# A Fourier layer and two MLPs on one core: conversions one step earlier, forward folds on VectorE, and more of the inverse split in halves

## The chip, the cores and the metric

The kernel runs on one core of a Trainium2 chip. The metric is the time of one execution on the device in microseconds; three runs of the kernel before stand below, and one profiled execution from which all rows come. The core's engines are TensorE (PE; its weight loads PEld), VectorE (DVE), ScalarE (ACT) and GpSimd (POOL); SyncE (SP) and GpSimd issue the DMAs. They work side by side and wait for each other through semaphores; each works through its own queue in order.

## What is computed

The input is two sequences of 3008 tokens with 256 channels, in float32. A Fourier transform over the tokens is followed by a complex 256x256 product, a bias, a soft threshold, and the inverse transform; its output goes through two MLPs, 256 to 2048 to 256, with float64 arithmetic nowhere but in the weights' storage.

```python
X = np.fft.rfft(x, axis=1)
Yr = Xr @ w_r - Xi @ w_i + b_r
Yi = Xr @ w_i + Xi @ w_r + b_i
Yr = np.sign(Yr) * np.maximum(np.abs(Yr) - 0.01, 0.0)    # Yi too
y = np.fft.irfft(Y, n=x.shape[1], axis=1)
h = y @ w_in;  g = h * sigmoid(1.702 * h);  z = g @ w_out
h = z @ w_in2; g = h * sigmoid(h);          out = g @ w_out2
```

## The kernel before

The program has four stages in a row.

**Forward** (`groups`, 16 steps g): the rfft as matrix products. The tokens are folded first: sums and differences of mirrored tokens (`fold`), so that the matrices shrink. A group (q, b, t) is a parity q of the sample, a batch b, and t, in which t // 2 is the parity of the frequency and t % 2 is cosine or sine. `fold(g + 3)` makes the operands `xf` of a later group: first `lv` (L309, 128x512) where t < 2, then `xf` or `dd` (L320, 128x256), and for q = 1 a further half (L329). `E(site, i)` picks the engine for each, V or P, from a string in CFG by index: in `lv` 5 and 11, in `dd` 10 and in `pr` 3 are P. `load_m` issues a group's matrix on SP, `load_raw` the next raw tiles. `fwd_mm(g)` multiplies (L361) and `fwd_evac` copies the result out of PSUM one step later.

**Middle** (`mids`, 12 steps i): the complex product (`mid_mm`: the first two in float32, L518, the others in three passes of rounded operands, L521, which need `wh` and `wl`, made at L502 and L503), then the threshold and the folds for the inverse.

**Inverse** (16 steps, 8q + 4b + t): `inv_mm` multiplies (L361, `psi`), `inv_post` adds and subtracts halves one step later. Where `split_sums` is true for a matrix, its rows are split into even and odd: two half-wide products give sums and differences, one copy on ScalarE (L648) and two adds on VectorE (L391, L656) join them. Where it isn't, ScalarE copies both banks (L643). CFG's `eo` has four digits for four matrices; the last is that of odd samples and even frequencies.

**MLPs** (two layers l, six blocks i of 1024 tokens, eight steps p each): `group` makes the hidden values of a pair of tiles by seven products (L818) with sums between (L837 and L853, L855 on ScalarE; L839, L863, L866 on VectorE), gates them (L821, L823, L828), and `out_next` adds the down products (L790) one step late. Between them it calls `hook(1)` to `hook(6)`.

The weights come as float64 bit patterns and are converted on the chip, in the order of `WEIGHTS`: `cv_load` fetches raw bits (SP; one buffer), `cv_bits` makes ScalarE's L175 and puts five VectorE operations (L180 to L184) and an accumulating DMA on GpSimd's queue (L185) into `fill`, which `pump` issues. The tile `cv_c` (tag `c`) has one buffer: the next L175 waits until that DMA has read it. `settle` collects what is converted; `place_in` and `place_out` (through `window`) split it into a rounded part and a rest (L105 to L110). Where these run is a list: `tf` steps of the forward stage, `tm` and `ml` of the middle, `ti` (convert) and `pl` (place) of the inverse, `kb` for the eight steps of the first MLP block and `kr` for later ones. Layer 0's sixteen pieces stay in SBUF; layer 1's are converted during later blocks, written to DRAM and fetched again.

Orders: in the forward stage GpSimd and SP keep program order and a planner orders the other engines; from the middle stage on all engines keep program order. PSUM has two pools of four banks.

Of the kernel before, what the change touches and what calls it, by code (L numbers as in the profile page):

```python
# [8 lines left out]

F32 = mybir.dt.float32  # L10
CFG = {'lv0': 'V', 'lv': 'VVVVVPVVVVVP', 'dd0': 'VPVVPPPPPVVP', 'dd': 'VVVVVVVVVVPV', 'ths': 'VVVVPV', 'thf': 'VVVP', 'ivf': 'V', 'cva': 'P', 'pol': 'PPPP', 'pil': 'P', 'mvl': 'PVVP', 'xl': 'V', 'xse': 'V', 'gl': 'VPPPPPPP', 'tf': [6, 9, 11, 14], 'tm': [1, 6, 10], 'ml': [4, 8], 'ti': [8, 11, 14], 'pl': [1, 4, 9, 12, 15], 'kb': [0, 1, 1, 1, 1, 1, 1, 0], 'kr': [0, 1, 0, 1, 0, 1, 1, 0], 'fa': 3, 'xp': [2, 4, 4, 5], 'xq': [1, 4, 1], 'xs': 4, 'xi': [7, 7, 9, 10, 10, 11, 8], 'xsi': 9, 'xo': (0, 1, 6, 2, 3, 4, 5), 'xd': (0, 1, 4, 6), 'ca': 4, 'tl': True, 'fwd': 'Pool,SP', 'rest0': 'all', 'rest1': 'all', 'last1': 'all', 'inv': 'all', 'mid': 'all', 'last0': 'all', 'thm': 'A', 'gl0': 'PVPVVVPV', 'gl2': 'PPPPPPPP', 'gl3': 'PPPPPPPV', 'xl0': 'V', 'xl1': 'V', 'pre': 14, 'pre2': 0, 'yd': 6, 'lvb': 6, 'mlp': 'all', 'pr': 'VVVP', 'pf': 'PV', 'eo': '0110', 'n32': 2, 'li': [8, 10, 11], 'lii': [0], 'xa': 4, 'nhb': 6, 'ddb': 6, 'mlp1': 'all', 'mlp2': 'all'}
NUM = dict(li=[5, 6, 7, 8], n32=2, pk=4, ydp=2, lii=[1, 3], xd=(), ml=[], pl=[], xo=range(7), pi=6, nhb=6, tf=[5, 9, 13], tm=[1, 3, 5, 7, 9, 11], ti=[0, 2, 4, 6, 8, 10, 12, 14, 14, 15, 15], kb=[2] * 8, kr=1, fa=3, fe=2, pm=0, nf=4, lvb=6, ddb=8, ivb=1, eob=1, fsb=6, f1=3, f2=0, fm=[7, 8, 9], fi=[1, 1, 2, 2], pre=13, pre2=1, yd=3, psh=0, ie=[12], xp=[1, 3, 4, 5], xq=[1, 2, 2], xs=5, nw=4, xi=[14, 14, 15, 15], xsi=13, rw=2, ca=4, cc=2, tb=1, tmn=1)

DEF = dict(pr="V", pf="V", lv0="V", lv="VPP", dd0="VVVVVP", dd="VPV", mpl="PV", ths="VP", thf="VVPP", fsl="VP", ivf="PPVV", cva="P", pol="P", pil="P", mvl="V", xl="PPVVPPP", xl0="PPVVPPP", xl1="PPVVPPP", xse="VP", gl="P", gl0="P", gl2="P", gl3="P", wcl="V", thc="V", thm="V")
# [7 lines left out]
P = 128  # L22
# [8 lines left out]
FS = 4  # L31

WEIGHTS = [("in", 0, p, True) for p in range(6)] + [("out", 0, p, True) for p in range(4)]
WEIGHTS += [(kind, 0, p, True) for kind, p in (("out", 4), ("out", 5), ("in", 6), ("in", 7), ("out", 6), ("out", 7))]
WEIGHTS += [(kind, 1, p, False) for kind in ("in", "out") for p in range(8)]

C_HI = float(np.uint32(0x0FEFFEF0).view(np.float32))
# [2 lines left out]
def split_sums(kind, q, p):  # L40
    return (kind, q) == ("f", 0) and CFG.get("eo", "1111")[p] == "1" or (kind, p) == ("i", 0) and CFG.get("eo", "1111")[2 + q] == "1"

# [14 lines left out]
def spectral_mlp_kernel(ctx, tc, xin, mfwd, minv, wc, bias, w_in1, w_out1, w_in2, w_out2, outT):  # L57
# [177 lines left out]
    def settle(now=False):  # L235
        pump()
        for u, (a, c) in bits:
            if not u[3]:
                spilled[u[:3]] = d = dram_p.tile([P, 2 * CU], F32, name=f"w_{u[0]}{u[1]}_{u[2]}")
                nc.sync.dma_start(out=d, in_=a)  # L240
        fresh = [(u, a) for u, (a, _) in bits if u[3]]
        done, added[:] = (added + fresh, ()) if now else (added[:], fresh)
        bits[:] = []
        return done
# [36 lines left out]
    raws, lvs, xs = {}, {}, {}  # L281
# [174 lines left out]

    prev = None
    for g, (q, b, t) in enumerate(groups):
        fold(g + N('fa'))
        ps = fwd_mm(g)  # L460
        if b == B - 1 and m_order[0][0] == "f":
            load_m()
        if prev is not None:
            fwd_evac(*prev)
        prev = (g, ps)
        if g == 6:
            wc_p = opened("wc", "right")
            wc_s = m_p.tile([P, MW], F32, tag="m", name="wc_s")[:, : 6 * D].rearrange("p (k d) -> p k d", k=2)
            bias_hl = wc_p.tile([P, 2 * D], F32R, name="bias_hl")
            bias_lo = wc_p.tile([1, 2 * D], F32R, name="bias_lo")  # L470
            bias_f = wc_p.tile([P, 2 * D], F32, name="bias_f")
            nc.gpsimd.memset(bias_f, 0.0)
            ones = wc_p.tile([P, P], F32R, name="ones")
            ones_f = wc_p.tile([P, P], F32, name="ones_f")

            neglam = wc_p.tile([P, 1], F32, name='neglam')
            nc.vector.memset(neglam, -LAM)


# [432 lines left out]
    done = []  # L912
    added.extend(hold)
    for at, (l, i, p) in enumerate(seq):
        if (l, i, p) in ((0, 0, 1), (0, 0, 2)):
            region(f'mlp{p}')
        if (i, p) == (1, 0):
            region(f'rest{l}')
        if (i, p) == (last, 0):
            region(f'last{l}')  # L920
        nxt = (l, i + 1) if i < last else (1, 0)
        more = p == NPR - 1 and (l, i) != (1, last)
        k = rate(at)

        def hook(h):
            if more:
                if h in (1, 2):
                    for x in ((0,), (1, 2))[h - 1]:
                        xprep(*nxt, x)
                if h == 3:  # L930
                    xprep(*nxt, 3, 1)
                if h == 4:
                    xprep(*nxt, 3, 2)
            if p == 0 and (l, i) != (0, 0):
                for x in {1: (4,), 3: (6, 5)}.get(h, ()):
# [12 lines left out]
            if h == 4:
                pump()
                cv_load(1 - len(loaded))  # L950
            if late and (l, i, p, h) in ((0, 0, 1, 4), (0, 0, 2, 3), (0, 0, 2, 4), (0, 0, 3, 4)):
                kk, y, u, v = late.pop(0)
                (nc.vector.tensor_sub if kk in (0, 3) else nc.vector.tensor_add)(y, u, v)
            if h == 3:
                pump()
                cv_load(1 - len(loaded))
                done.extend(settle())
                done.extend(added)
                added[:] = []
# [146 lines left out]
```

## Time and profile before

| | us |
|---|---|
| runs of the kernel before | 1184.57, 1178.29, 1178.03 |
| their median | 1178.29 |
| profiled execution, whole | 1182.72 |
| its span, first to last instruction | 1180.6 |
| TensorE busy in the span | 1150.5 (97%) |
| ScalarE busy | 773.3 (65%) |
| VectorE busy | 636.1 (54%) |
| GpSimd busy | 502.4 (43%) |

The stages can be read from the lines: the forward stage ends at about 73 us, the middle at about 147, the inverse at about 196; the first MLP block ends near 279. Busy shares are means over stages with different limits, so each stage is read by itself.

### The profile page before, as it was taken

How to read it: one execution, taken by the hardware profiler on the slowest of the kernel's cores; microseconds unless marked ns; L12 is line 12 of the kernel's file. 1: busy time of each engine (PE TensorE's matmuls, PEld its weight loads, DVE VectorE, ACT ScalarE, POOL GpSimd, SP SyncE). 2: the span in 40 equal slices, each digit the busy share in tenths (PEclk: the TensorE clock that was granted, in tenths of full speed). 3: DMA queues.
4: the chain of work that ended last, by engine and by line, in shares of the span. 5: the costliest groups of instructions: out<-in, count | busy, mean ns of one | idle time of the engine just before them, and what ended most of it. 6: DMA issues, size and time to landing. Idle time of an engine off the chain costs nothing.

```text
span 1180.6 us, 14536 instructions
## 1 busy us (share of the span) xinstructions
PE 1150.5 (97%) x5052; PEld 945.3 (80%) x5052; DVE 636.1 (54%) x987; ACT 773.3 (65%) x1439; POOL 502.4 (43%) x430
## 2 busy tenths in 40 slices
PE   7889998999999999999999999999999999999998
PEld 4658885877888888888889978888888888888897
DVE  7768787776556466365564553352532623523522
ACT  2366545777668667667677787675665766766755
POOL 2355254443444444344446755433333433433333
PEclk9989999999999999999999999999999999999999
DMA  7457478432121221121130200010000000000000
GB/s 270 142 128 148 126 148 163 89 80 45 44 64 36 72 63 37 45 72 37 36 89 5 68 10 27 1 37 1 1 36 1 11 26 1 36 1 1 36 1 31
DMA packets 37835, 66.83 MB, mean 57 GB/s; under 512 B 3457, under 2 KB 14977, under 8 KB 37762
## 3 DMA queue, kind: packets, MB, share of 16 engines
q1 hardware_dynamic: 25730, 45.90, 11.9%
q0 software_dynamic: 12032, 20.01, 9.8%
q8 instruction: 39, 0.64, 0.2%
q14 instruction: 34, 0.28, 0.1%
HBM read 35.53 MB, written 10.35 MB: 39 GB/s over the span
## 4 chain that ended last, share of the span: by engine, by line
PE 76%; ACT 3%; DVE 2%; issue 1%; DMA 0%; DVEq 0%; POOL 0%; POOLq 0%
PE o L790 40%; PE x L818 36%; ACT yt L821 1%; DMA wo<-cv_a 0%; ACT x L727 0%; ACT yt L837 0%; DVE yt L839 0%; DVE tmp L213 0%; DVE yt L863 0%; ACT g L823 0%; DVE x L734 0%; ACT yt L855 0%; ACT yt L853 0%; DVE g L828 0%; DVE cv_a L182 0%
## 5 line engine op out<-in xcount | busy, mean ns | idle before, releaser
L828 POOL TENSOR_TENSOR g<-yt,g 128x512 fp32r<-128x512 f32 (+1 forms) x282 | 362.8, 1299 | 491.4 <-PE x L818 337.1
L790 PE MATMUL o<-g,wo 128*128 128x512 f32 (+1 forms) x2304 | 561.0, 386 | 2.6 <-DMA wo<-cv_a 2.6
L818 PE MATMUL x<-x,wi 128*128 128x512 f32 (+1 forms) x2016 | 501.2, 388 | 7.8 <-ACT yt L837 3.1
L790 PEld LDWEIGHTS o<-g,wo 128*128 128x128 f32 x2304 | 433.0, 188 | 83.8 <-DMA wo<-cv_a 3.1
L818 PEld LDWEIGHTS x<-x,wi 128*128 128x128 f32 x2016 | 378.2, 188 | 86.1 <-ACT yt L837 5.4
L821 ACT ACTIVATE yt<-yt 128x512 f32<-128x512 f32 (+1 forms) x288 | 179.1, 622 | 257.1 <-DVE yt L863 205.8
L823 ACT CAST g<-yt 128x512 fp32r<-128x512 f32 (+1 forms) x384 | 235.1, 612 | 12.2
L863 DVE TENSOR_TENSOR yt<-yt,x 128x512 f32<-128x512 f32 (+1 forms) x96 | 64.7, 674 | 217.2 <-PE x L818 216.7
L839 DVE TENSOR_TENSOR yt<-yt,x 128x512 f32<-128x512 f32 (+1 forms) x96 | 64.8, 675 | 167.4 <-ACT yt L837 167.4
L828 DVE TENSOR_TENSOR g<-yt,g 128x512 fp32r<-128x512 f32 (+1 forms) x102 | 70.1, 688 | 72.1 <-ACT g L823 72.1
L361 PE MATMUL psf<-m,xf 128*128 128x190 f32 (+3 forms) x224 | 57.7, 419 | 15.7 <-DVE xf L320 6.5
L361 PEld LDWEIGHTS psf<-m,xf 128*128 128x128 f32 x224 | 41.7, 204 | 31.1 <-POOL xf L320 7.9
L866 DVE TENSOR_TENSOR yt<-yt,x 128x512 f32<-128x512 f32 (+1 forms) x96 | 64.8, 675 | 0.0
L734 DVE TENSOR_TENSOR x<-yt,x 128x512 fp32r<-128x512 f32 (+1 forms) x44 | 46.1, 1047 | 29.7 <-ACT x L727 29.7
L185 POOL DMA_DIRECT2D cv_a<-cv_c x32 | 28.0, 875 | 77.5 <-DVE cv_c L184 61.4
L855 ACT COPY yt<-x 128x512 f32<-128x512 f32 (+1 forms) x96 | 55.8, 581 | 0.7 <-ACT yt L853 0.6
L821 ACT ACTIVATE yt<-x 128x512 f32<-128x512 f32 (+1 forms) x96 | 56.2, 585 | 0.0
L853 ACT COPY yt<-x 128x512 f32<-128x512 f32 (+1 forms) x96 | 55.0, 572 | 0.0
L837 ACT COPY yt<-x 128x512 f32<-128x512 f32 (+1 forms) x96 | 54.8, 571 | 0.0
L361 PE MATMUL psi<-m,f 128*128 128x376 f32 (+3 forms) x208 | 49.9, 396 | 0.0
L361 PEld LDWEIGHTS psi<-m,f 128*128 128x128 f32 x208 | 36.6, 190 | 11.9
L175 ACT ACTIVATE cv_c<-raw 128x512 f32<-128x512 f32 x32 | 21.6, 675 | 27.3 <-DMA cv_a<-cv_c 27.1
(117 smaller groups left out, 834.0 us busy)
## 6 DMA issues: line engine op xcount, KB each, us to landing
raw<-in_wi SPq DMA_DIRECT2D x32, 256.0 KB, 3.5
cv_a<-cv_c POOLq DMA_DIRECT2D x32, 256.0 KB, 5.0
raw<-in_wo SPq DMA_DIRECT2D x16, 512.0 KB, 4.0
raw<-in_x SPq DMA_DIRECT2D x12, 512.0 KB, 4.8
xl<-xt POOLq DMA_DIRECT2D x20, 256.0 KB, 5.5
out_t<-yt SPq DMA_DIRECT2D x20, 256.0 KB, 2.2
m<-in_mi SPq DMA_DIRECT2D x4, 564.0 KB, 9.1
wo<-cv_a POOLq DMA_DIRECT2D x8, 256.0 KB, 5.5
```

The source lines that it names most:

```text
L361: nc.tensor.matmul(ps, hi[:, c : c + P], m[:, k, :w], start=i == 0, stop=i == last)
L790: nc.tensor.matmul(acc[h, mm], st, mv, start=first and k == 0, stop=last and k == 2)
L818: nc.tensor.matmul(ps, st, mv, start=first and m == 0, stop=m == 2, skip_group_check=True)
L821: nc.scalar.activation(g, g if src is None else src, func)
L823: nc.scalar.copy(gh, g)
L828: eng.tensor_sub(gl, g, r32(gh))
L837: nc.scalar.copy(y1, X)
L839: nc.vector.tensor_add(y1, y1, Y)
L853: nc.scalar.copy(y2, Z)
L855: nc.scalar.copy(y3, X)
L863: nc.vector.tensor_add(y2, y2, X)
L866: nc.vector.tensor_add(y3, y3, Z)
```

## The change

Six things, all in the first 285 us or in what is issued there.

- `lv`, `dd` and `pr` become V throughout: three L309, four L320 and two L329 move from GpSimd to VectorE (the early ones of `dd0` stay).
- In the forward loop `fwd_mm(g)` and `load_m` come before `fold(g + 3)`; on SP the matrix load then stands before the raw loads of that fold.
- `eo` is 0111 in place of 0110: the inverse's matrix of odd samples and even frequencies is (4, 188) in place of (3, 376), in steps 8, 9, 12 and 13.
- Conversions: `tm` and `ml` one step earlier, `pk` 6 in place of 4 (a conversion's operations pumped in one middle step), `ti` 5, 8, 11 in place of 8, 11, 14, `pl` with a step 7 more, `kb` one step earlier (its first conversion, that of down piece 4, now in step 0).
- In step 0 of the MLPs that conversion starts at hook 4 in place of 1 and is settled there, so that it can be placed in step 1.
- `WEIGHTS`: down piece 6 before the up pieces 6 and 7.

```diff
-CFG = {'lv': 'VVVVVPVVVVVP', 'dd': 'VVVVVVVVVVPV', 'pr': 'VVVP', 'eo': '0110',
-       'tm': [1, 6, 10], 'ml': [4, 8], 'ti': [8, 11, 14], 'pl': [1, 4, 9, 12, 15],
-       'kb': [0, 1, 1, 1, 1, 1, 1, 0]}
+CFG = {'lv': 'V', 'dd': 'V', 'pr': 'V', 'eo': '0111',
+       'tm': [1, 5, 9], 'ml': [3, 7], 'pk': 6, 'ti': [5, 8, 11], 'pl': [1, 4, 7, 9, 12, 15],
+       'kb': [1, 1, 1, 1, 1, 1, 0, 0]}
...
-WEIGHTS += [(kind, 0, p, True) for kind, p in (("out", 4), ("out", 5), ("in", 6), ("in", 7), ("out", 6), ("out", 7))]
+WEIGHTS += [(kind, 0, p, True) for kind, p in (("out", 4), ("out", 5), ("out", 6), ("in", 6), ("in", 7), ("out", 7))]
...
     for g, (q, b, t) in enumerate(groups):
-        fold(g + N('fa'))
         ps = fwd_mm(g)
         if b == B - 1 and m_order[0][0] == "f":
             load_m()
+        fold(g + N('fa'))
...
-            if h == 1:
+            if h == (1 if at else 4):
                 window(k, ())
...
             if h == 4:
                 pump()
                 cv_load(1 - len(loaded))
+                if at == 0:
+                    done.extend(settle(True))
```

## Rows read from the trace of the kernel before

**Rows 1.** Stages: stretch and its length, busy us (instructions) by engine, clock, DMA

```profile
core 0: us, PE busy (x) PEld busy (x) DVE busy (x) ACT busy (x) POOL busy (x), PEclk, DMA share, GB/s
...
62.00:74.00 12.00, 6.28 (x20) 5.28 (x20) 8.44 (x18) 5.66 (x14) 7.22 (x8) 0.72 0.52 110
74.00:147.00 73.00, 73.00 (x299) 55.45 (x298) 60.14 (x110) 47.94 (x82) 30.35 (x32) 1.00 0.62 135
147.00:196.00 49.00, 49.00 (x213) 36.83 (x212) 40.45 (x75) 23.83 (x46) 25.12 (x25) 1.00 0.83 157
...
285.00:1180.00 895.00, 889.23 (x3984) 746.60 (x3982) 422.14 (x604) 614.23 (x1109) 384.75 (x306) 1.00 0.11 31
```

**Rows 2.** TensorE's waits before 300 us: total, times, longest

```profile
PE psf L361 <- POOL xf L320: 6.2, 3, 5.5
PE x L818 <- ACT yt L837: 3.0, 1, 3.0
PE psf L361 <- DMA m<-in_mf: 2.8, 1, 2.8
PE o L790 <- DMA wo<-cv_a: 2.6, 1, 2.6
```

**Rows 3.** Timeline, forward tail to third middle step: start, us, engine, line [idle before]

```profile
61.24 0.69 ACT L175 ACTIVATE cv_c<-raw 128x512 f32<-128x512 f32 x1 [7.42 <-DMA cv_a<-cv_c]
...
66.92 0.87 POOL L185 DMA_DIRECT2D cv_a<-cv_c  x1 [2.03 <-DVE cv_c L184]
...
68.61 4.75 PE L361 MATMUL psf<-m,xf 128*128 128x188 f32 x14 [5.49 <-POOL xf L320]
...
80.14 1.75 DVE L503 TENSOR_TENSOR wl<-wc_s,wh 128x1536 fp32r<-128x1536 f32 x1
...
86.99 0.80 PE L521 MATMUL psm<-wh,xh 128*128 128x512 f32 x1
```

**Rows 4.** VectorE's folds before 210 us by form: count, busy us, mean ns, idle

```profile
L309 DVE TENSOR_TENSOR lv<-raw 128x512 f32<-128x512 f32 x10 | 6.5, 686 | 0.8 <-DMA raw<-in_x 0.8
...
L320 DVE TENSOR_TENSOR dd<-lv 128x256 f32<-128x256 f32 x8 | 3.0, 420 | 0.1
```

**Rows 5.** Two stretches of the inverse: half-wide forms, then 376-wide ones

```profile
156.00:166.00 10.00, 10.00 (x62) 9.75 (x61) 8.46 (x21) 3.88 (x7) 5.56 (x6) 1.00 1.05 231
...
176.00:186.00 10.00, 10.00 (x33) 6.03 (x32) 9.02 (x17) 5.41 (x12) 5.37 (x6) 1.00 1.01 183
```

**Rows 6.** Timeline of VectorE in the inverse and at the first MLP step

```profile
151.30 1.76 DVE L184 SCALAR_TENSOR_TENSOR cv_c<-raw,cv_c 128x512 f32<-128x512 uint32 x1
...
163.60 0.55 DVE L391 TENSOR_TENSOR rt<-psi,eo 128x376 f32<-128x376 f32 x1
...
199.20 0.43 DVE L180 TENSOR_SCALAR cv_c<-cv_c 128x512 f32<-128x512 f32 x1 [4.90 <-ACT cv_c L175]
...
204.59 0.68 DVE L863 TENSOR_TENSOR yt<-yt,x 128x512 f32<-128x512 f32 x1
```

**Rows 7.** Timeline of MLP steps 0 and 1; last, the landing of L185's 32 DMAs

```profile
208.26 0.59 ACT L821 ACTIVATE yt<-x 128x512 f32<-128x512 f32 x1
...
209.89 0.67 ACT L175 ACTIVATE cv_c<-raw 128x512 f32<-128x512 f32 x1
...
212.42 0.59 ACT L855 COPY yt<-x 128x512 f32<-128x512 f32 x1
...
213.58 1.52 PE L818 MATMUL x<-x,wi 128*128 128x512 f32 x6
...
213.94 0.87 POOL L185 DMA_DIRECT2D cv_a<-cv_c  x1 [2.96 <-DVE cv_c L184]
...
DMA to landing us min/median/max: 3.3/5.0/9.4
```

**Rows 8.** Timeline of TensorE: the nine products at the turn of a step

```profile
226.50 2.20 PE L818 MATMUL x<-x,wi 128*128 128x512 f32 x9
...
236.70 2.20 PE L818 MATMUL x<-x,wi 128*128 128x512 f32 x9
...
269.40 2.26 PE L818 MATMUL x<-x,wi 128*128 128x512 f32 x9
...
284.11 2.20 PE L818 MATMUL x<-x,wi 128*128 128x512 f32 x9
```

More of the change, by code (lines that the diff above doesn't have):

```diff
@@ L10 @@
 F32 = mybir.dt.float32
-CFG = {'lv0': 'V', 'lv': 'VVVVVPVVVVVP', 'dd0': 'VPVVPPPPPVVP', 'dd': 'VVVVVVVVVVPV', 'ths': 'VVVVPV', 'thf': 'VVVP', 'ivf': 'V', 'cva': 'P', 'pol': 'PPPP', 'pil': 'P', 'mvl': 'PVVP', 'xl': 'V', 'xse': 'V', 'gl': 'VPPPPPPP', 'tf': [6, 9, 11, 14], 'tm': [1, 6, 10], 'ml': [4, 8], 'ti': [8, 11, 14], 'pl': [1, 4, 9, 12, 15], 'kb': [0, 1, 1, 1, 1, 1, 1, 0], 'kr': [0, 1, 0, 1, 0, 1, 1, 0], 'fa': 3, 'xp': [2, 4, 4, 5], 'xq': [1, 4, 1], 'xs': 4, 'xi': [7, 7, 9, 10, 10, 11, 8], 'xsi': 9, 'xo': (0, 1, 6, 2, 3, 4, 5), 'xd': (0, 1, 4, 6), 'ca': 4, 'tl': True, 'fwd': 'Pool,SP', 'rest0': 'all', 'rest1': 'all', 'last1': 'all', 'inv': 'all', 'mid': 'all', 'last0': 'all', 'thm': 'A', 'gl0': 'PVPVVVPV', 'gl2': 'PPPPPPPP', 'gl3': 'PPPPPPPV', 'xl0': 'V', 'xl1': 'V', 'pre': 14, 'pre2': 0, 'yd': 6, 'lvb': 6, 'mlp': 'all', 'pr': 'VVVP', 'pf': 'PV', 'eo': '0110', 'n32': 2, 'li': [8, 10, 11], 'lii': [0], 'xa': 4, 'nhb': 6, 'ddb': 6, 'mlp1': 'all', 'mlp2': 'all'}
+CFG = {'lv0': 'V', 'lv': 'V', 'dd0': 'VPVVPPPPPVVP', 'dd': 'V', 'ths': 'VVVVPV', 'thf': 'VVVP', 'ivf': 'V', 'cva': 'P', 'pol': 'PPPP', 'pil': 'P', 'mvl': 'PVVP', 'xl': 'V', 'xse': 'V', 'gl': 'VPPPPPPP', 'tf': [6, 9, 11, 14], 'tm': [1, 5, 9], 'ml': [3, 7], 'pk': 6, 'ti': [5, 8, 11], 'pl': [1, 4, 7, 9, 12, 15], 'kb': [1, 1, 1, 1, 1, 1, 0, 0], 'kr': [0, 1, 0, 1, 0, 1, 1, 0], 'fa': 3, 'xp': [2, 4, 4, 5], 'xq': [1, 4, 1], 'xs': 4, 'xi': [7, 7, 9, 10, 10, 11, 8], 'xsi': 9, 'xo': (0, 1, 6, 2, 3, 4, 5), 'xd': (0, 1, 4, 6), 'ca': 4, 'tl': True, 'fwd': 'Pool,SP', 'rest0': 'all', 'rest1': 'all', 'last1': 'all', 'inv': 'all', 'mid': 'all', 'last0': 'all', 'thm': 'A', 'gl0': 'PVPVVVPV', 'gl2': 'PPPPPPPP', 'gl3': 'PPPPPPPV', 'xl0': 'V', 'xl1': 'V', 'pre': 14, 'pre2': 0, 'yd': 6, 'lvb': 6, 'mlp': 'all', 'pr': 'V', 'pf': 'PV', 'eo': '0111', 'n32': 2, 'li': [8, 10, 11], 'lii': [0], 'xa': 4, 'nhb': 6, 'ddb': 6, 'mlp1': 'all', 'mlp2': 'all'}
 NUM = dict(li=[5, 6, 7, 8], n32=2, pk=4, ydp=2, lii=[1, 3], xd=(), ml=[], pl=[], xo=range(7), pi=6, nhb=6, tf=[5, 9, 13], tm=[1, 3, 5, 7, 9, 11], ti=[0, 2, 4, 6, 8, 10, 12, 14, 14, 15, 15], kb=[2] * 8, kr=1, fa=3, fe=2, pm=0, nf=4, lvb=6, ddb=8, ivb=1, eob=1, fsb=6, f1=3, f2=0, fm=[7, 8, 9], fi=[1, 1, 2, 2], pre=13, pre2=1, yd=3, psh=0, ie=[12], xp=[1, 3, 4, 5], xq=[1, 2, 2], xs=5, nw=4, xi=[14, 14, 15, 15], xsi=13, rw=2, ca=4, cc=2, tb=1, tmn=1)
```

## The prediction

> **What bounds the kernel now.** I read the stage table first [rows 1]. From 285 us on TensorE is busy 889 of 895 us at full clock, and the change edits nothing there: three quarters of the run is out of reach. What can move lies before 285 us. Next come TensorE's own waits in that part [rows 2]: 5.5 us in one piece for a fold on GpSimd, 2.8 us for a matrix load, 3.0 us for ScalarE at the start of the first MLP step, 2.6 us for a down weight. The last readings are of the engines around each of these places [rows 3 to 8].
>
> *The forward tail.* The last forward group waits for one half-fold that GpSimd may start only after a conversion's accumulating DMA (L185 at 66.92) because GpSimd keeps program order [rows 3]. That DMA waits for VectorE's bits, these for L175 at 61.24, and L175 sat 7.42 us until the conversion before it had landed: `cv_c` has one buffer. So conversions form a chain, and each L175 in it holds ScalarE's queue. TensorE resumes at 68.61 and runs 14 matmuls in 4.75 us, 0.34 us each, with the granted clock at 1.2 GHz for a while (the stretch's mean is 0.72 of 2.4 GHz [rows 1]); forms of this width otherwise start every 0.161 us [rows 5], so 2.5 us are lost after the wait.
>
> *The inverse.* TensorE is busy all 49 us of 147 to 196 [rows 1], but VectorE runs behind it: the last inverse work and the first MLP adds reach it only at 204 (L863 at 204.59), after 4.90 us behind ScalarE's L175 [rows 6], the same one-buffer chain.
>
> **The change, part by part.**
>
> *Folds off GpSimd.* Three 128x512 and six 128x256 operations move to VectorE: 3 x 0.69 + 6 x 0.42 = 4.6 us more there [rows 4]. The 5.5 us wait loses its cause. Late next is the conversion chain, since ScalarE still holds what follows L175 (the remaining evacuations, the spectral weights) and VectorE still holds `wl` (L503, 80.14 + 1.75 = 81.9 us), without which the third middle step cannot run; it ran at 86.99 [rows 3]. The chain itself starts a little earlier: VectorE no longer waits for GpSimd's folds, but takes its work over; I put 1.5 us. Then `wl` is there at 80.4 and the third middle step gains 6.5 us. From there to 196 TensorE shows no idle time [rows 1], so the gain is kept up to the inverse's second half. Bounds: if all 4.6 us push the chain, 0.4 us are left; if nothing but TensorE's own waits counted (6.2 for GpSimd's folds and 2.8 for the matrix [rows 2], and the clock's 2.5), 11.5 us. I take 6.5, because `wl` is a named wait between them.
>
> *Loads before the folds.* SP now issues a group's matrix before the next raw tiles. The 2.8 us wait for `in_mf` [rows 2] should go; it lies inside the 11.5 above and is covered by the same chain, so it adds nothing.
>
> *Inverse split.* Four steps (odd samples, even frequencies, two batches) change from 6 products of 376 columns to 8 of 188; each product is two records. 48 records at 33 per 10 us are 14.5 us, 64 at 62 per 10 us are 10.3 us [rows 5]: 4.2 us off TensorE. ScalarE loses a 376-wide copy per step, VectorE gains two PSUM adds of 0.55 us [rows 6], 8 x 0.55 = 4.4 us, on the engine that is already late.
>
> *Conversions earlier.* One conversion leaves the inverse's end (the 4.90 us go) and one joins its middle; their number there stays three. The last one of the middle stage is pumped in one go, so L184 at 151.30 (1.76 us) leaves the inverse's start [rows 6]. VectorE's end of the inverse: -4.9 + 4.4 - 1.8 = -2.3 us. But ScalarE now places the third of these down weights right before the first MLP copies: the conversion ends twelve 0.55 us operations before VectorE's end, about 195.2, its DMA lands 5.0 us later (median, [rows 7]), then come two placing operations and three copies of 0.59 us: 203.2 at best, and one product more before L863, which so stays near 204.6. Bounds: -4.2 (TensorE's gain passes through) to +4.9 (the DMA takes 9.4 us, the longest of [rows 7]). I take +0.5.
>
> *Two conversions close together.* This is the edit that adds a wait. Step 0 now converts at its fourth hook and step 1 at its first. On ScalarE the fourth hook lies where L821 starts at 208.26; from L175 to its DMA's issue take 4.05 us (209.89 to 213.94), landing 5.0 us more [rows 7]: `cv_c` is free at 217.3. Step 1's L175, which ran at 209.89, comes to the head of ScalarE's queue one such instruction later, near 210.6, and stands there 6.7 us. Queued behind it are the first gate, the copies L853 and L855, and so the fifth product. L855 ends 3.1 us after L175 starts [rows 7], hence 220.4, where this product ran at 213.58: 6.8 us late. TensorE finishes what is queued before that product, idles some 6 us, and loses clock as after the 5.5 us wait, 2.5 us: +9.3 us. The steps behind it are 10.2 us apart, a conversion's round 9.05, so it happens once. Bounds by the landing's extremes: 3.3 gives 7.6, 9.4 gives 13.7.
>
> The Trainium skill (DMA: Bandwidth & Descriptors, section Anatomy of one DMA — SWDGE (gpsimd) path) gives a fixed 2.0 us and the bytes over 436 GB/s, an estimate of 2.6 us for 256 KB; no row here shows that, the shortest landing being 3.3, and by it step 1 would cost 6.9 and the sum be 2.4 us less.
>
> *The down weight `out6`.* It was placed in step 6 behind step 6's own conversion on GpSimd's queue and was wanted at step 7's start. It is now placed in step 3, and step 6 has no conversion. The step that held this wait took 284.11 - 269.40 = 14.7 us, its neighbours 236.70 - 226.50 = 10.2 [rows 8]: -4.5 us. `out7`, placed in step 6, is wanted in block 1.
>
> *Sum*: -6.5 + 0.5 + 9.3 - 4.5 = -1.2 us. The profiled execution took 1182.7 us (span 1180.6 and 2.1 around), 4.4 above the median of the runs shown; 1181.5 there is 1177.1 at the median's level.
>
> **Rivals.**
>
> *A: the inverse's TensorE time reaches the end* (VectorE keeps pace): -4.2 in place of +0.5, 1172.4. For it: no wait of TensorE in the stage. Against it: 8 us of VectorE's lag at 204, and 4.4 us added.
>
> *B: step 1's wait is short*, because the DMA finds a free queue (3.3 us) or TensorE has more queued: 1175.4 with the shortest landing, 1167.8 if it costs nothing. Against it: the 3.0 us wait at 200 [rows 2] came of the same cause, 4.9 us at VectorE [rows 6], of which TensorE felt more than half. The page's 2.6 us belongs here: 1174.7.
>
> *C: the forward gain is whole*: the chain moves with TensorE and all waits go, -11.5 in place of -6.5, 1172.1. For it: chain and loads start earlier together. Against it: the chain runs through VectorE, which gets the folds.
>
> *D, on the other side: the folds push the conversion chain on VectorE.* Place: VectorE between 16 and 43 us, ahead of the first conversion's L184. Price: 0.4 gained in place of 6.5, so 1183.2, slower than before; it decides from the point where the third middle step gains less than 5.3 us.
>
> *E: nothing is felt*, each gain lying under another wait: 1178.3, inside the forecast's range.
>
> **Numbers.** Forecast with E 0.45 (its own range 1173 to 1182), A 0.12, B 0.16, C 0.15, D 0.12. A change of 1% (11.8 us, about what a measurement of this kernel can tell from none) needs two of A, B and C together for faster, below 1166.5: 0.18 by the weight that these have in common, since an earlier chain helps all three. Slower by 1%, above 1190, needs D and the 9.4 us landing at once: 0.06. Within 1%: 0.76. The range 1165 to 1186 reaches from two of A, B, C together to D with a landing a few us late, leaving 2 in 10 outside.
>
> **What would show each step.** No TensorE wait on GpSimd's folds; the first L521 of the middle stage near 80.5. 188-wide forms in the inverse's second half, TensorE waiting there for VectorE's adds, and L863 of step 0 about 6 us earlier than 204.59, by the forward gain alone. In step 1 a ScalarE wait of L175 for `cv_a<-cv_c` of 5 to 7 us, with TensorE idle before the fifth product and at low clock after it. Step 7 at 10.2 us. Wrong: an L175 in step 1 that does not wait, a first L521 at 86 or at 75, or an inverse without TensorE waits.

## The result: slower by 1.1%, and the forward stage is where the forecast went wrong

| | kernel before | changed kernel |
|---|---|---|
| median of 6 runs each, same chip, us | 1179.97 | 1194.35 (1191.04 to 1195.71) |
| ratio, 95% interval | 1 | 1.0112 [1.0083, 1.014] |
| profiled execution's span, us | 1180.6 | 1193.1 |

The forecast was 1177.1 with a range of 1165 to 1186, and "slower by over 1%" had 6 in 100. The profiled spans differ by 12.5 us, so the trace holds nearly all of the 14 us. TensorE's waits of the changed kernel before 300 us (us in total, times, longest), beside [rows 2]:

```profile
PE x L818 <- ACT yt L855: 6.8, 2, 6.1
PE psf L361 <- DVE xf L320: 6.5, 2, 6.3
PE x L818 <- ACT yt L837: 5.5, 1, 5.5
PE psm L518 <- ACT wc_s L339: 3.9, 1, 3.9
PE psm L524 <- DMA bias_hl<-bias_lo: 3.7, 1, 3.7
PE psf L361 <- DMA m<-in_mf: 2.9, 1, 2.9
PE psi L361 <- DVE rt L391: 1.8, 1, 1.8
PE psm L521 <- DMA xl<-xt: 1.7, 2, 1.1
...
PE psm L521 <- ACT xh L454: 0.9, 1, 0.9
```

The 5.5 us for a fold on GpSimd and the 2.6 us for a down weight are gone; new are 3.9 for `wc_s`, 3.7 for `bias_hl`, 2.6 in the middle stage for `xl` and `xh`, 2.6 in the inverse for `rt`, and 6.1 at `L855`. The 6.5 us for folds on VectorE stood in the kernel before too, nearly all of it ahead of the first product. Where the 12.5 us stand, by the same event in both traces:

| event | before | after | late by | this stretch adds | forecast |
|---|---|---|---|---|---|
| first middle product (L518) | 73.15 | 67.57 | -5.6 | -5.6 | |
| third middle step (first L521) | 86.99 | 89.99 | +3.0 | +8.6 | -6.5 for both |
| inverse begins (first `psi`) | 144.56 | 151.07 | +6.5 | +3.5 | 0 |
| step 0's L863 | 204.59 | 213.33 | +8.7 | +2.2 | +0.5 |
| nine products at the end of step 1 | 216.30 | 233.39 | +17.1 | +8.4 | +9.3 |
| the same at the end of step 7 | 284.11 | 296.65 | +12.5 | -4.6 | -4.5 |

Three of the four terms of the sum came out. The first is 13 us off: -6.5 was forecast up to the inverse's start, +6.5 is there. The places of it, from the timeline of the changed kernel, one line for each (start, us, engine, line, [idle before]):

```profile
45.23 1.00 POOL L185 DMA_DIRECT2D cv_a<-cv_c  x1 [32.90 <-DVE cv_c L184]
52.96 0.68 ACT L175 ACTIVATE cv_c<-raw 128x512 f32<-128x512 f32 x1 [5.83 <-DMA cv_a<-cv_c]
58.62 0.87 POOL L185 DMA_DIRECT2D cv_a<-cv_c  x1 [2.04 <-DVE cv_c L184]
65.13 0.67 ACT L175 ACTIVATE cv_c<-raw 128x512 f32<-128x512 f32 x1 [8.64 <-DMA cv_a<-cv_c]
66.47 1.05 ACT L339 COPY wc_s<-wc_f 128x1024 f32<-128x1024 f32 x1
67.57 5.40 PE L518 MATMUL psm<-wc_s,xt 128*128 128x512 f32 x8 [3.94 <-ACT wc_s L339]
71.49 0.87 POOL L185 DMA_DIRECT2D cv_a<-cv_c  x1 [1.31 <-DVE cv_c L184]
72.08 0.81 POOL L344 DMA_DIRECT2D bias_hl<-bias_lo  x1
76.69 0.77 PE L524 MATMUL psm<-bias_hl,ones 128*128 128x512 f32 x1 [3.73 <-DMA bias_hl<-bias_lo]
77.26 9.62 PE L518 MATMUL psm<-wc_s,xt 128*128 128x512 f32 x16
89.99 0.80 PE L521 MATMUL psm<-wh,xh 128*128 128x512 f32 x1
```

The same places in the kernel before, beside [rows 3]:

```profile
43.14 1.00 POOL L185 DMA_DIRECT2D cv_a<-cv_c  x1 [4.05 <-DVE cv_c L184]
68.20 0.81 POOL L344 DMA_DIRECT2D bias_hl<-bias_lo  x1
73.15 3.64 PE L518 MATMUL psm<-wc_s,xt 128*128 128x512 f32 x8
76.23 0.79 PE L524 MATMUL psm<-bias_hl,ones 128*128 128x512 f32 x1
76.86 7.03 PE L518 MATMUL psm<-wc_s,xt 128*128 128x512 f32 x16
```

TensorE is done with the forward stage at 67.57 - 3.94 = 63.6 us, some 9.5 earlier than it began the middle stage before. It then waits for `wc_s`: L339 stands on ScalarE behind an L175 that stood 8.64 us for the transfer of the conversion before it. The load that L339 reads is late too: SP issues it at 59.32, right behind the next raw bits (58.38), whose one buffer the second conversion leaves at 58.3, and it lands 7.0 us later, at 66.3 (before: issued at 56.28, 5.3 us). So ScalarE's queue and SP's each hold L339 until about 66. And TensorE waits for `bias_hl`: its small transfer stands on GpSimd behind L185. In the kernel before the three transfers went out at 43.14, 55.58 and 66.92 (the last in [rows 3]); here at 45.23, 58.62 and 71.49, so the chain of conversions is later by 2.1, 3.0 and 4.6 us. It was moved behind TensorE's need, while TensorE moved ahead.

The clock adds to it. Granted clock of TensorE in the same 15 us, changed kernel and, in the second fence, kernel before (columns as in [rows 1], TensorE alone):

```profile
68.00:83.00 15.00, 11.27 (x17) 0.66 0.77 150
```

```profile
68.00:83.00 15.00, 14.39 (x38) 0.83 0.59 135
```

After each of the two waits the clock is at 1.2 GHz for a while: the first eight products take 5.40 us and the next sixteen 9.62; in the kernel before they took 3.64 and 7.03. From 67.57 to 89.99 the changed kernel takes 22.42 us where 13.84 stood: 3.73 of the difference is the bias, and the other 4.85 goes with the clock: in steps of half a microsecond it stands at 0.50 under some 9.4 us of this work, which by estimate costs half of that, 4.7.

At the MLPs' start (timeline of the changed kernel):

```profile
207.57 0.63 ACT L105 ACTIVATE wo<-cv_a 128x512 fp32r<-128x512 f32 x1 [3.64 <-DMA cv_a<-cv_c]
209.25 1.65 PE L818 MATMUL x<-x,wi 128*128 128x512 f32 x3 [5.49 <-ACT yt L837]
225.87 0.66 ACT L175 ACTIVATE cv_c<-raw 128x512 f32<-128x512 f32 x1 [7.07 <-DMA cv_a<-cv_c]
228.72 1.65 PE L818 MATMUL x<-x,wi 128*128 128x512 f32 x3 [6.10 <-ACT yt L855]
...
286.45 2.20 PE L818 MATMUL x<-x,wi 128*128 128x512 f32 x9
...
296.65 2.20 PE L818 MATMUL x<-x,wi 128*128 128x512 f32 x9
```

This is what was forecast: step 1's L175 waits 7.07 us (forecast 6.7) for step 0's transfer, issued at 220.95, the fifth product waits behind it, and step 7 takes 296.65 - 286.45 = 10.2.

### The profile page after: what moved, and what is told of

It is laid out like the page before. It is cut to its first block, busy times and chain, and to the rows that moved or that the text cites. A ratio compares the mean times of both kernels' runs of the same rounds, so it can differ in the third digit from the quotient of the medians.

```text
span 1193.1 us, 14567 instructions
## 1 busy us (share of the span) xinstructions
PE 1150.0 (96%) x5068; PEld 946.3 (79%) x5068; DVE 635.9 (53%) x1003; ACT 771.2 (65%) x1435; POOL 493.4 (41%) x422
## 3 DMA queue, kind: packets, MB, share of 16 engines
q1 hardware_dynamic: 25730, 45.51, 11.7%
## 4 chain that ended last, share of the span: by engine, by line
PE 77%; DVE 3%; ACT 3%; issue 3%; DMA 2%; POOL 1%; DVEq 0%; POOLq 0%; ACTq 0%
PE o L790 40%; PE x L818 35%; DMA cv_a<-cv_c 1%; DMA xl<-xt 1%; ACT yt L821 1%; PE psi L361 1%; PE psm L521 1%; ACT x L727 0%; POOL yt L702 0%; ACT yt L837 0%; DVE ac L667 0%; DVE rt L668 0%; POOL g L828 0%; ACT g L823 0%; DVE tmp L213 0%
## 5 line engine op out<-in xcount | busy, mean ns | idle before, releaser
L818 PEld LDWEIGHTS x<-x,wi 128*128 128x128 f32 x2016 | 379.2, 189 | 95.3 <-ACT yt L855 12.2
L823 ACT CAST g<-yt 128x512 fp32r<-128x512 f32 (+1 forms) x384 | 235.2, 612 | 12.2
L863 DVE TENSOR_TENSOR yt<-yt,x 128x512 f32<-128x512 f32 (+1 forms) x96 | 64.8, 674 | 220.8 <-PE x L818 220.2
L185 POOL DMA_DIRECT2D cv_a<-cv_c x32 | 28.0, 875 | 117.8 <-DVE cv_c L184 96.9
L361 PE MATMUL psf<-m,xf 128*128 128x190 f32 (+3 forms) x224 | 54.3, 403 | 9.4 <-DVE xf L320 6.5
L855 ACT COPY yt<-x 128x512 f32<-128x512 f32 (+1 forms) x96 | 55.7, 580 | 1.3 <-PE x L818 1.3
L837 ACT COPY yt<-x 128x512 f32<-128x512 f32 (+1 forms) x96 | 54.6, 569 | 0.0
L361 PE MATMUL psi<-m,f 128*128 128x188 f32 (+3 forms) x224 | 45.7, 358 | 2.8 <-DVE rt L391 1.8
L175 ACT ACTIVATE cv_c<-raw 128x512 f32<-128x512 f32 x32 | 21.5, 672 | 35.0 <-DMA cv_a<-cv_c 32.3
```

The lines of the kernel that those rows point to most:

```text
L361: nc.tensor.matmul(ps, hi[:, c : c + P], m[:, k, :w], start=i == 0, stop=i == last)
L818: nc.tensor.matmul(ps, st, mv, start=first and m == 0, stop=m == 2, skip_group_check=True)
L823: nc.scalar.copy(gh, g)
L837: nc.scalar.copy(y1, X)
L855: nc.scalar.copy(y3, X)
L863: nc.vector.tensor_add(y2, y2, X)
```

## The experiments

Two theories for the forward stage. **The chain**: one `cv_c` buffer ties each conversion to the transfer before it, ScalarE's and GpSimd's queues stand behind that, and TensorE meets the chain wherever the first instruction behind it is wanted. **VectorE**: the folds that came from GpSimd take its time ahead of or between the conversion's operations (rival D). For the MLPs' start each suspected edit was taken back alone. Ratios are to the kernel before on the same chip and at the same time (its medians there: 1180.6 beside the four kernels of part 1; 1182.1 beside `early_wc`, `inv_only`, `step0_h1` and `no_pl15`; 1181.1 beside `dve_order`, `best1`, `best4` and `best6`; 1181.6 beside the rest). One profiled execution lies up to 5 us from the median of its kernel's runs, so totals are read from ratios and places from profiles.

**1. The forward edits one at a time.**

`f_folds`, on the kernel before:

```diff
-'lv': 'VVVVVPVVVVVP', 'dd': 'VVVVVVVVVVPV', 'pr': 'VVVP'
+'lv': 'V', 'dd': 'V', 'pr': 'V'
```

> The kernel before with one edit: the nine late forward folds on VectorE. Prediction's theory (the 5.5 us wait of TensorE goes and the conversion chain starts 1.5 us earlier): third middle step (first L521) near 80.5 us, time -6.5 us against before. Rival theory (the folds push the conversions on VectorE, so that the chain of L185 and with it the spectral weights and the bias come later): L185 of the first conversion 1 to 2 us later than 43.14, bias landing later than 73.4, first L521 between 87 and 90, time between 0 and +3 us. Third theory (the loads' order is what made the chain late): this run gains the 6.5 us.

`f_order`, on the kernel before:

```diff
-        fold(g + N('fa'))
         ps = fwd_mm(g)
         if b == B - 1 and m_order[0][0] == "f":
             load_m()
+        fold(g + N('fa'))
```

> The kernel before with one edit: in the forward loop the products and the matrix load stand before the fold, so that SP issues the matrix before the raw tiles. Theory that the folds push the chain: the 2.8 us wait for the matrix goes, the tail keeps its 5.5 us wait for GpSimd, first L521 between 84 and 87, time between -3 and 0 us. Theory that the loads' order made the chain late: first L521 at 89 or later, time +3 us.

`undo_fwd`, the changed kernel with both of these taken back:

> The changed kernel with its two forward edits undone (folds and order as before), all else as changed. If the forward part costs what the trace shows at the third middle step (89.99 against 86.99), the time falls by 3.0 us; if the middle stage's lateness (3.5 us more up to the inverse) also comes from the forward part, it falls by 6.5 us; if the forward part as a whole is a gain hidden by the bias, it stays.

`undo_mid`, the changed kernel with `'tm': [1, 6, 10], 'ml': [4, 8]` and no `pk`, as before:

> The changed kernel with the middle stage's lists as before (conversions in steps 1, 6, 10, loads in 4 and 8, four operations pumped at a time). Theory that a conversion pumped in one piece delays the threshold on VectorE and with it the operands of a later step: the three TensorE waits for xh and xl between 131 and 141 us (2.65 us in all) go, the inverse starts 3 us rather than 6.5 us later than before, time -3.5 us against the changed kernel. Rival (the waits come of the matrix loads' DMAs, or of the forward stage): the waits stay and so does the time.

| kernel | median us | ratio | third transfer issued | inverse begins, against before |
|---|---|---|---|---|
| f_folds | 1184.39 | 1.0034 [1.0018, 1.0051] | 71.03 | +1.6 |
| f_order | 1178.65 | 0.9987 [0.9971, 1.0003] | 65.71 | -2.9 |
| undo_fwd (the lists stay) | 1184.83 | 1.0041 [1.0024, 1.0059] | 67.95 | +1.8 |
| undo_mid (both forward edits stay) | 1192.27 | 1.0097 [1.0072, 1.0122] | 71.07 | +1.9 |

The folds alone cost time; the order alone costs none. `f_folds` came out as its rival theory, a little stronger (first L521 at 88.57, time 3.8 us up), `f_order` as the folds' theory (first L521 at 84.10, time 1.9 us down). `undo_mid` lost the waits for `xh` and `xl`, but only about 2 us of time in place of 3.5. `undo_fwd` gained more than any of its three cases, 8 to 10 us, of which its profile shows 4.7 up to the inverse's start; the rest isn't shown.

Kernels that are alike up to the inverse show how far a single profile can be off: the changed kernel, `step0_h1` and `no_pl15` (below) begin it at 151.07, 153.42 and 149.34, the kernel before and `inv_only` at 144.56 and 143.25. The last column thus carries some 2 us either way: +1.6, +1.8 and +1.9 can't be told apart, while the +6.5 of the whole is clear. Folds alone, order alone and lists alone add to +0.5 there, all three together give +6.5; that they cost more together is likely, but why isn't shown. With the folds on VectorE the third transfer goes out at 70 to 72 us with either order and either lists, without them at 65 to 68, and the waits for `wc_s` and `bias_hl` stand in both kernels that have them there (1.9 and 4.0 us in `f_folds`, 2.1 and 5.7 in `undo_mid`), in `undo_fwd` neither. So the folds make the chain late; the earlier lists seem to cost on top.

**2. The first thing behind the chain taken out of it.** `early_wc`, the changed kernel:

```diff
-        if g == 10:
+        if g == 7:
             load_wc()
-        if g == 13:
+        if g == 10:
             prep_wc()
+        if g == 13:
```

> The changed kernel with the spectral weights and the bias loaded at forward step 7 and prepared at step 10, in place of 10 and 13, so that the bias' DMA no longer stands behind the third conversion's on GpSimd's queue. Theory that the first middle step's waits for wc_s and bias_hl (3.9 and 3.7 us, and the clock lost after them) are what turned the forward gain into a loss: both waits go, the first L521 comes near 82 us in place of 90, time -6 to -8 us against the changed kernel. Rival (the conversion chain itself, through wl or VectorE, holds the third middle step): the wait moves to another operand and less than 3 us are gained.

1188.77 us, 1.005 [1.0034, 1.0067]: 6.7 us above the kernel before, in place of 14.4. Both waits are gone and the third middle step begins at 80.55, where the forecast had it (80.5). But the inverse still begins at 147.52: TensorE now waits 5.4 us for `xh` (ScalarE) and 2.5 for `xl`. ScalarE stands 6.88 us for the fourth conversion's transfer, until its L175 at 88.70, and makes the first late `xh` at 100.48: the wait went on to later users of the same queues.

**3. VectorE in program order.** `dve_order`, the changed kernel with `'fwd': 'Pool,SP,DVE'`: the planner doesn't place VectorE's forward work.

> The changed kernel, with one difference: in the forward stage VectorE's instructions keep the order in which the program lists them; the planner doesn't place them. Theory O (the folds hold up the conversion because of where VectorE's order puts them, ahead of the conversion's own operations): the last accumulating transfer of the chain (line 185, 71.5 us in the changed kernel) is issued at 66 to 68 us, the waits for wc_s and bias_hl (3.9 and 3.7 us) fall to under 2 us together, and the time is 3 to 7 us under the changed kernel's 1194.4: about 1189. Theory D (the chain is late because its transfers land late, whatever VectorE's order): line 185 stays at 70.5 to 72.5 and the time within 2 us of the changed kernel's. Theory S (VectorE simply has no room for the folds: 12 to 14 us more of work between the second product and the middle stage): the conversion comes early, but the folds come late, a new wait of TensorE on a fold of 3 us or more stands in the last forward steps, and the time is no better.

1189.09 us, 1.0068 [1.0044, 1.0093]. The total is where theory O had it, but not for its reason: the transfers go out at 46.66, 59.46 and 70.43, so the first two are later still, and the last gained 1.1 us, not 3.5 to 5.5.

```profile
46.66 1.00 POOL L185 DMA_DIRECT2D cv_a<-cv_c  x1 [32.20 <-DVE cv_c L184]
59.46 0.87 POOL L185 DMA_DIRECT2D cv_a<-cv_c  x1 [2.04 <-DVE cv_c L184]
70.43 0.87 POOL L185 DMA_DIRECT2D cv_a<-cv_c  x1 [2.04 <-DVE cv_c L184]
73.07 0.54 POOL L344 DMA_DIRECT2D bias_hl<-bias_lo  x1 [1.77 <-DVE ones_f L345]
```

(Timeline of GpSimd in this run.) What changed is that the bias's transfer went out later, 2.6 us behind L185, and landed sooner (2.9 us after its issue against 4.5); TensorE waited 0.4 us for it. In program order the first pass of the chain holds no folds (L175 at 41.52, L184 at 45.66: 4.1 us, in place of 10.4 in the changed kernel), but it begins 7.6 us later, with the folds ahead of it and a wait of 4.70 us for its raw bits. The order decides where the delay stands; with the folds on VectorE the chain was late in both. Of theory S's sign, a new wait for a fold, 2.6 us for L329 are there, but at 28 us and not in the last steps.

**4. The chain cut.** `noacc_after` and `noacc_before`, the changed kernel and the kernel before without the accumulating transfers of the first four conversions:

```diff
-                lambda: nc.gpsimd.dma_start(out=a, in_=c, accum_op=ALU.add),
             )
         )
+        ncv.append(1)
+        if len(ncv) > 4:
+            fill.append(lambda: nc.gpsimd.dma_start(out=a, in_=c, accum_op=ALU.add))
```

> The changed kernel without the accumulating transfers (line 185) of the first four weight tiles that it converts, in the forward stage and at the start of the middle one; the low parts of these tiles are left out of the result. Theory D (the landings of 6.4 to 7.7 us, one behind the other with one cv_c buffer, hold up ScalarE's queue, and with it wc_s and bias_hl behind it): wc_s and bias_hl are ready before TensorE wants them, the 3.9 and 3.7 us of waits go, the clock doesn't fall after them, the first line-521 product begins at 77 to 81 instead of 90.0, the inverse at 138 to 143 instead of 151.1, and the time is 9 to 13 us under the changed kernel's. Theory O (VectorE's folds between lines 181 and 184 hold it up): the three passes still take 5.7 to 10 us of VectorE each; wc_s comes early all the same, but TensorE waits 2 us or more for late folds, and less than half of this gain comes.

> The kernel before without the same transfers (line 185) of the first four weight tiles; the low parts of these are left out of the result. In the kernel before, TensorE waited in the middle stage for none of this: the 5.5 us wait for a fold on GpSimd stood ahead and hid it. So the first line-521 product stays at 85.5 to 87.5 us, the inverse's start at 143 to 145, the time within 2 us of the kernel before. If the forecast's step was right and only these transfers kept it from coming out, the changed kernel without them begins the inverse 5 to 7 us earlier than this one. If it begins at the same time or later, the step itself failed: the fold's wait was not worth 5.5 us.

`noacc_after`: 1181.45 us, 0.9997 [0.9987, 1.0007]; `noacc_before`: 1173.95 us, 0.9932 [0.9913, 0.9951]. TensorE's waits before 300 us, the longest of the changed kernel without the transfers, then of the kernel before without them (line numbers are 4 higher in both):

```profile
PE psf L365 <- DVE xf L324: 7.4, 2, 6.4
PE x L822 <- ACT yt L859: 6.4, 2, 5.7
PE x L822 <- ACT yt L841: 3.3, 1, 3.3
PE psm L525 <- DMA xl<-xt: 2.6, 2, 2.0
```

```profile
PE psf L365 <- DVE xf L324: 6.3, 1, 6.3
PE x L822 <- ACT yt L841: 3.0, 1, 3.0
PE psf L365 <- DMA m<-in_mf: 2.4, 1, 2.4
```

In the changed kernel all of it comes as the chain's theory had it: no wait for `wc_s` or `bias_hl`, clock 1.00 from 38 to 145 us, the third middle step at 77.02 in place of 89.99, the inverse at 138.55 in place of 151.07. In the kernel before the expectation failed, and this is the most useful miss: it was to stay as it was, and the third middle step begins at 78.78 in place of 86.99, the inverse at 136.36 in place of 144.56, 8.2 us earlier. Its 5.5 us wait for a fold *on GpSimd* is gone too, with the fold still on GpSimd. That fold had been late because it stood on GpSimd's queue behind L185 [rows 3]; it was the chain that TensorE felt there, through another instruction. The edit takes 1 MB of transfers out as well, so a part of the gain may be room for other transfers; that isn't separated. Without the chain the two kernels' third middle step differs by 78.78 - 77.02 = 1.8 us in favour of the change, and at the inverse's start by 2.2 against it (2.6 for `xl`, 0.4 for `xh`). The forecast's -6.5 is in neither number.

**5. The inverse's split, and the MLPs' start.**

`inv_only`, on the kernel before: `'eo': '0111'` for `'0110'`.

> The kernel before with one edit: the inverse's matrix of odd samples and even frequencies split in halves. Theory of the prediction (VectorE, late already, gets 4.4 us more; TensorE's 4.2 us don't come through): TensorE waits in the inverse's second half for VectorE's adds, L863 of the first MLP step between 204.6 and 209, time 0 to +4 us against before. Rival A (TensorE's time comes through): time -4 us.

1182.58 us, 1.0009 [0.999, 1.0028]: nothing. TensorE now waits 1.8 and 0.8 us for VectorE's `rt`, 4.0 instead of 3.0 for L837, and L863 of step 0 stands at 204.56 (204.59 before), though the inverse began 1.3 us earlier in this profile.

`step0_h1`, the changed kernel with step 0's conversion at the second slot again:

```diff
-            if h == (1 if at else 4):
+            if h == 1:
```

> The changed kernel with the conversion in MLP step 0 started at hook 1 in place of hook 4, some 9 us earlier and a full step ahead of the next. Theory that the two conversions stand too close for one cv_c and one raw buffer: ScalarE's wait of 7.1 us at step 1's L175 and TensorE's 6.1 us go, time -8 us against the changed kernel. Rival (the wait is the raw load's or the order's and moves into step 0): no more than 3 us are gained.

1184.64 us, 1.0016 [1.0003, 1.0028]. The 6.1 us wait for L855 is 0.7. In its profile the inverse begins 2.3 us later than in the changed kernel's (5.9 us for `bias_hl` where that had 3.7), and yet step 1 ends at 228.19 in place of 233.39: from L863 to there it takes 12.8 us in place of 20.1 (11.7 in the kernel before), 7.2 of the 8 us expected. By the runs it stands 2.6 us above the kernel before in place of 14.4, which is 11.8 less. Where the rest was gained isn't shown; the changed kernel's 14.4 has an interval of 9.8 to 16.5.

`no_pl15`, the changed kernel with the 15 left out of `pl`, so that the last piece is placed in MLP step 1:

> The changed kernel with the last placing of the inverse (step 15, the fourth down piece) left to MLP step 1. Theory that ScalarE's wait for this piece's DMA (3.6 us before L105) is what holds the first MLP copies: TensorE's 5.5 us wait for L837 shrinks to 2 us or less, L863 of step 0 comes 2 to 4 us earlier, time -2 to -4 us against the changed kernel. Rival (VectorE's end of the inverse holds step 0 anyway): L863 moves by less than 1 us, and so does the time.

1188.59 us, 1.0051 [1.0033, 1.007], 6.5 above the kernel before. The wait for L837 falls from 5.5 to 0.9 us, and L863 comes 57.4 us after the inverse's start in place of 62.3; the wait for L855 stays at 6.1. The two waits are separate.

**6. Put together.** `best1` is the changed kernel with `early_wc`, `step0_h1` and `no_pl15`; `best4` with the folds on GpSimd as before (the order stays new), `step0_h1` and `no_pl15`; `best6` is `best4` with the middle lists as before; `best5` is `best4` with the early load; `best4_noeo` is `best4` with `'eo': '0110'`.

> The changed kernel with three things put back or moved together: the load and the first operation of the middle weights' conversion three and six forward groups earlier (alone 1188.8), the conversion in MLP step 0 at the second slot again (alone 1184.6), and the last inverse placing left to MLP step 1 (alone 1188.6). If the three delays are separate and stand one behind the other on TensorE's path, their gains add: 5.6 from the first, 6.1 from the wait on line 855 of the second, 4.6 from the wait on line 837 of the third, 16.3 under 1194.9: a span's time of 1178 to 1179. If the second and the third are one queue (line 837 and line 855 wait for the same ScalarE stretch), only the larger counts: 1182 to 1184. If what goes early turns into waits in the middle stage again (xh 5.4 and xl 2.5 in the run with the early load), the inverse still begins at 147 and later, and nothing of this gets below the kernel before (1180).

> The changed kernel with the late forward folds on GpSimd as before (the fold still behind the products and the load, as changed), the conversion in MLP step 0 at the second slot, and the last inverse placing left to MLP step 1. What is left of the change: the moved fold, the earlier middle conversion and placing lists, and the split of odd samples and even frequencies. If the folds on VectorE are the cause of the forward loss (13 us between forecast and trace up to the inverse's start), the last line-185 transfer of the chain is issued near 65.7 us, the inverse starts at 142 to 144 us, and the time is 1170 to 1174, under the kernel before. If the earlier middle lists cost as much by themselves (xh and xl waits), the inverse starts at 145 or later and the time is 1176 to 1180, no better than before.

> The kernel of the run just above, and the middle stage's two lists as in the kernel before as well: of the change only the moved fold, the split, and the earlier later-step conversions are left. If the lists' advance is worth something once the conversion chain is early (the forecast's minus 1 at most), this is within 1 us of the run above: 1171 to 1175. If the lists' advance costs 2 us as it did in the changed kernel (1192.3 against 1194.4 without it), this is 2 us under the run above. The inverse starts at 141.5 to 143 in both of these cases.

> The kernel with the folds on GpSimd as before, the conversion in MLP step 0 at the second slot and the last inverse placing left to MLP step 1 (1177.2 us), and with the middle weights loaded and first converted earlier as well. If wc_s and bias_hl still hold TensorE there (no such wait stands in that kernel's trace), 3 us more come: 1174. If that chain is no bound any longer, the early load brings nothing and only takes room from the other transfers: 1176 to 1180, with a wait on xh or xl of 1 us or more as in both other runs with the early load.

> The kernel with the folds on GpSimd as before, the conversion in MLP step 0 at the second slot and the last inverse placing left to MLP step 1 (1177.2 us), with the inverse's steps split as in the kernel before (those of odd samples and even frequencies whole). If the split of these steps is worth nothing, as in the kernel before with this edit alone (1182.6 against 1182.1), the time is within 1.5 us of 1177. If it is worth what TensorE saves by it less the waits on line 391 (1.8 and 0.8), it is 1 to 3 us slower without it.

| kernel | median us | ratio to the kernel before |
|---|---|---|
| best1 | 1179.55 | 0.9994 [0.9979, 1.001] |
| best4 | 1177.19 | 0.9964 [0.9947, 0.998] |
| best6 | 1177.89 | 0.9985 [0.9967, 1.0003] |
| best5 | 1177.96 | 0.9958 [0.9942, 0.9974] |
| best4_noeo | 1175.10 | 0.9941 [0.9921, 0.9961] |

`best1` is 1.6 us under the kernel before where the changed kernel was 14.4 over: 16 us, near the 16.3 expected. That doesn't show that the three gains add: the 16.3 put one difference of times beside two waits, and alone the three edits gained 7.7, 11.8 and 7.9 us, 27 together. By the events of the two profiles `best1` gains 3.4 us up to the inverse's start, 2.0 from there to L863 (where `no_pl15` alone gained 4.9) and 6.4 to the end of step 1, 11.9 in all.

`best4` is faster than both kernels, by 0.4% against the kernel before, though short of the 1170 to 1174 expected. Its waits name neither `wc_s` nor `bias_hl`, but the chain is still there. TensorE waits 12.2 us for folds on VectorE, 5.4 of them at the end of the forward stage, for one that stands on VectorE's queue right behind the third conversion's L184 (timeline of `best4`):

```profile
65.68 0.69 DVE L184 SCALAR_TENSOR_TENSOR cv_c<-raw,cv_c 128x512 f32<-128x512 uint32 x1
66.29 0.42 DVE L320 TENSOR_TENSOR xf<-keep 128x256 f32<-128x256 f32 x1
66.86 0.96 PE L361 MATMUL psf<-m,xf 128*128 128x188 f32 x2 [5.38 <-DVE xf L320]
```

`best6` begins the inverse at 139.41 where `best4` begins it at 143.29, but L863 follows at 202.33 and 203.15 and the medians differ by 0.7 us: nearly all of this lead is gone by L863, and what took it isn't shown. The early load brings nothing once the folds are off VectorE, and the split nothing either: without it the kernel is no slower, and has the lowest median (the two were run at different times, and their intervals overlap). Two `cv_c` buffers, which would loosen the chain itself, weren't tried.

## Why the prediction failed, step by step

**Folds off GpSimd: wrong, and it decides.** Two things in "The 5.5 us wait loses its cause. Late next is the conversion chain" need mending. The prediction had read from [rows 3] that the fold starts only after L185; experiment 4 shows that this was the whole of the wait: the fold was a messenger of the chain, and with it taken away the chain reached TensorE by SP's load of the spectral weights, ScalarE's L339 and GpSimd's L344 instead. And what is late next was named wrongly. I took `wl`, because it is needed for the third step; in the changed kernel L503 is done at 78.6, 11 us before that step. The first two middle steps need `wc_s` and `bias_hl`, and they come first. The rows for that were in the trace of before: the bias's transfer, issued at 68.20, landed 5.2 us later, at 73.4, and was wanted at 76.2. There were 2.8 us of room, and the forecast moved TensorE by 5.5.

**The chain's own shift: wrong sign.** It was put 1.5 us earlier; it came 2.1 to 4.6 later. The first L175 did start earlier (33.88 against 36.36), but from there to L184 it then took 10.4 us where it had taken 5.8, since the planner put 23 folds between L180 and L184 where 5 had stood. At most six of these came from GpSimd; most are folds that VectorE ran before as well, nine or ten of them (`xf<-keep`) only after L184 (timeline of VectorE in the changed kernel):

```profile
34.91 0.42 DVE L180 TENSOR_SCALAR cv_c<-cv_c 128x512 f32<-128x512 f32 x1
...
37.92 0.42 DVE L181 TENSOR_SCALAR cv_c<-cv_c 128x512 uint32<-128x512 uint32 x1
38.26 1.43 DVE L320 TENSOR_TENSOR xf<-lv 128x256 f32<-128x256 f32 x4
39.60 1.76 DVE L320 TENSOR_TENSOR xf<-keep 128x256 f32<-128x256 f32 x5
41.28 0.69 DVE L182 SCALAR_TENSOR_TENSOR cv_a<-raw,cv_c 128x512 uint32<-128x512 uint32 x1
41.88 1.43 DVE L320 TENSOR_TENSOR xf<-keep 128x256 f32<-128x256 f32 x4
43.22 0.42 DVE L183 TENSOR_SCALAR cv_c<-cv_a 128x512 uint32<-128x512 uint32 x1
43.56 0.76 DVE L320 TENSOR_TENSOR xf<-keep 128x256 f32<-128x256 f32 x2
44.23 0.69 DVE L184 SCALAR_TENSOR_TENSOR cv_c<-raw,cv_c 128x512 f32<-128x512 uint32 x1
```

That is 2.1 of the 4.6. Another 1.0 came from the first landing, 0.9 from the second (65.13 - 58.62 = 6.5 us from issue to the next L175, before 61.24 - 55.58 = 5.7), and 0.7 from the third pass. Kernels with the same forward stage differ by up to 1.6 us at the third transfer (69.92 to 71.56), so the parts of 1 us and less aren't resolved, and how much of the longer landings is VectorE's doing isn't shown. Rival D named the mechanism, the place and the side. Its price was too small: +0.4 of gain left at the third step, where +3.0 of loss stood. It counted the chain's delay, and neither the clock after the waits (4.85 us here) nor the waits for `wc_s` and `bias_hl` themselves.

**Kept to the inverse's second half: wrong.** "From there to 196 TensorE shows no idle time, so the gain is kept" is a statement on the kernel before. It says nothing of how much room `xh` and `xl` had. The changed kernel waits for both, 2.6 us; with the lists put back (`undo_mid`) these waits are gone, and the early load made them longer. The change adds 3.5 us from the third middle step to the inverse, and 4.0 even without the chain (experiment 4: from 1.8 ahead to 2.2 behind).

**Loads before folds: half.** It was to add nothing to the forward gain. `f_order` has no wait for `in_mf` left, and begins the inverse 2.9 us earlier; TensorE waits 0.3 us for the bias there, so the room of 2.8 us is used up. With the folds on VectorE the wait for `in_mf` is 2.9 us still.

**Inverse split and hand-over: right.** +2.2 against +0.5, inside -4.2 to +4.9. TensorE waits for `rt` as forecast, so VectorE bounds the end and the 4.2 us of TensorE stay there (`inv_only`): from the first `psi` to the first MLP product it takes 49.2 us with 2.8 us of waits, 50.7 without any before. The landing of the last piece before the first MLP copies was in the forecast; ScalarE stands 3.64 us for it, and it can be avoided by one placing less (`no_pl15`).

**Two conversions close together: right,** +8.4 against +9.3, at the place and by the wait forecast (7.07 against 6.7 us), undone by the edit that it was put down to. **`out6`: right,** -4.6 against -4.5. For the two conversions the Trainium skill (DMA: Bandwidth & Descriptors, section Anatomy of one DMA — SWDGE (gpsimd) path), with its fixed 2.0 us and 436 GB/s, would have given an estimate of 2.6 us a landing and 6.9 for the term. The trace doesn't agree: the shortest landing of these transfers in the changed kernel is 3.9 us, the median 4.9.

**The range.** It was a sum of one-sided cases: D and a long landing were to be together before the time passed 1190. The forward term was given 6.1 us of room on the bad side (0.4 of gain in place of 6.5); it used 13.

## What to carry to other kernels

When an engine's wait ends on an instruction that stands behind another queue's stall, the releaser named is only the messenger: follow the queue in front of it, and before moving that instruction to another engine, list what else stands behind the same stall and when each is wanted. As here, a gain of so many microseconds on the bounding engine can be worth no more than the smallest slack among the things that it will now want earlier; read those slacks from the trace of before (here 2.8 us on a bias of 2 KB). And when an engine that carries a latency chain takes over work, look at what then runs ahead of and between the chain's operations, not at its share of busy time: VectorE was 54% busy before and 53% after, and the chain's first pass went from 5.8 to 10.4 us.

## What the hardware showed

- Around waits of 3.7 to 5.5 us TensorE's granted clock fell from 2.4 to 1.2 GHz for a part of the work behind them (0.50 of full speed from 68 to 72 us in the kernel before, 0.50 to 0.69 in three of the four stretches of 4 us from 68 to 84 us in the changed kernel). Two waits of 3.9 and 3.7 us in the changed kernel were followed by products that together took 4.85 us longer than the same ones in the kernel before.
- The bias's 2 KB landed 4.1 to 6.6 us after their issue in the fourteen traces in which they were issued up to 1.3 us behind a 256 KB accumulating transfer on GpSimd's queue, and 2.3 to 4.1 us after it in the four in which that one was over 2.6 us ahead or absent.
- Taking four transfers of 256 KB (the low parts of four weight tiles) out of the kernel before took 8.2 us off the inverse's start, and 0.7% off the whole, with the engines' other work as it was (the result lacks these low parts).
